# Late linear attention in 64-token chunks of two batches, fused with a cosine MLP

## The chip, the cores and the metric

The kernel runs on one core of one Trainium2 chip. The metric is the device time of the program in microseconds. TensorE (PE) does the matrix products, VectorE (DVE) and ScalarE (ACT) the elementwise work and the copies out of PSUM, GpSimd (POOL) part of the elementwise work that stays in SBUF, and the DMA queues of SyncE (SP), ACT and POOL move data.

## The reference

Two layers, one behind the other. The first is a linear attention with a decaying state, for 4 batches, 8 heads, 768 tokens and a head size of 48:

```python
for t in range(S):
    cur = u * k_t v_t^T
    y[t] = r_t (state + cur)
    state = w[:, None] * state + k_t v_t^T
```

The second takes its 3072 tokens of 384 values through an MLP of 2048 hidden values: `h = x @ w_in`, `g = h * cos(h)`, `out = g @ w_out`. The weights come as 64-bit floats.

## The kernel before

**Attention.** A batch's 768 tokens are cut into 6 chunks of C = 128; there are 24 chunks, taken round the batches, chunk `i` being batch `i % 4`, part `i // 4` (`chunk`, L656 on). In a chunk the decay is written as powers of w: k and r are multiplied by tables `decT_k` and `decT_r` (head dimension on partitions, time along the free axis, `spread_decay` L454, spread at L456), so that the scores of all pairs of tokens are plain products kT·rT (`mm_a` L815). A diagonal matrix with the bonus u goes into `A` on ACT (`diagonal` L805), and DVE writes the scores of earlier tokens over it (`mask` L825, a predicated copy). The chunk's output x, transposed, is the sum of the state read (`mm_x` L835, state `zt` against rT) and the values (`mm_x2` L845, v against A), in one PSUM bank; ACT and DVE copy it out as a high and a low half (`x_h`, `x_l`, L914, L919). The state product (`mm_z` L871, k against v) and its decay (`state` L926) make the state for the batch's next chunk. Heads are kept in pairs of 48 padded to 64 rows, so two score products stand on two halves of the array, four state reads and values on four strips of 32 columns. All of these are float32 products.

The first 12 chunks (XS) load k and r by tokens and transpose them on PE. The later ones ("late", `i >= XS`) load a second, staged copy of k and r and transpose it on DVE in 32x32 blocks (`load_s` L690, `tr_s` L735), and POOL applies the decay tables (`decay_s` L742). A late chunk issues its scores as one block on PE (`o_A` L821) and the state read, values and state product as a second (`mm_xz` L879).

**The tables.** `powers` (L442) takes w, transposed by PE, clamps it, forms 24 powers in seven multiplications, takes their reciprocals, and makes two factor tables `qk` and `qr` with one more product `cq`; DVE spreads both into `decT_k` and `decT_r`. PE transposes `decT_k` back into `dec_k` (tokens on partitions) for the state product. w is loaded by the first DMA on SP's queue (L430).

**The MLP.** Tokens go in 8 blocks of 3 chunks. One step takes a block and 128 of the 2048 hidden values: 9 products for h (`mm_h` L316, 384 columns, each operand split in a high and a low part), then on ACT and DVE the cosine (`whole` L327, `rest` L330, `cosine` L333), the gate g = h·cos(h) (`f_gate` L1030), and g's high and low halves (`f_gh` L1033, `f_gl` L1036), then 9 products for the output (`mm_o` L322). Blocks 0 to 3 walk the hidden dimension together in four groups, while their weights are converted (`conv` L564 on); blocks 4 to 7 take all of it at once and are stored once each.

**Order.** Nothing is issued in the order of the code. Each piece of work is an `Op` with an engine, a cost, a latency, a due time and the buffers it needs; `Plan.order` lays them out by a greedy pass, and repeats that with changed due times (PASSES = 60), replaying each order with random delays and keeping the best. A buffer is a `Buf` that takes one of several `Tile`s when its first user is placed; the eight PSUM banks are such tiles: `B_ACC` three, `B_H` two for h (three, `B_HX`, in the first four blocks), `B_ATT` three for late attention. While PE would idle ahead of the first score product, the plan puts warm-up matmuls on a zero tile (L1094).

## Time and profile before

| what | value |
|---|---|
| median of 3 runs (lowest, highest) | 512.46 us (512.25, 513.9) |
| the profiled execution's own time | 512.26 us |
| its span, first to last instruction | 510.5 us |
| mean granted PE clock | 0.999 |
| PE busy | 501.5 us, 98% |
| DVE busy | 381.0 us, 75% |
| ACT busy | 331.0 us, 65% |
| POOL busy | 177.1 us, 35% |

A row of the timeline has the start, the time from the first start to the last end, the engine, the line of the kernel, the operation, the tile written, the tiles read, the shapes, the count of merged instructions and, in brackets, the idle time before and what ended it. Weight loads of PE stand on rows of their own (PEld). A row of the windows has the window, its length, each engine's busy time with its count, the granted clock, the DMA share and the GB/s. A row of the groups has the count, the busy time and the mean of one in ns, then the idle time before.

### The profile page before, as it was taken

Reading aid. Unit: us, or ns where it says so; the run is one execution under the profiler, and the core shown is the slowest. Engines: PE = TensorE matmul, PEld = TensorE weight load, DVE = VectorE, ACT = ScalarE, POOL = GpSimd, SP = SyncE. Lnnn points to the kernel's source line nnn. Section 1 sums busy time; section 2 is a strip of 40 time slices with the busy share of each in tenths; the row PEclk is TensorE's granted clock in tenths of the full one; section 3 lists DMA queues with packets and bytes.
Section 4 is the critical chain, followed back from the end, with each engine's and each line's share of the span. In section 5 each row is a group of like instructions: output and inputs, shape, how many; then the busy total and the mean of one; then the engine's idle time right before and its main releaser. Section 6 shows DMA issues by size and latency. Waiting matters only on the chain.

```text
span 510.5 us, 11742 instructions
## 1 busy us (share of the span) xinstructions
PE 501.5 (98%) x4389; PEld 480.0 (94%) x4389; DVE 381.0 (75%) x773; ACT 331.0 (65%) x833; POOL 177.1 (35%) x184
## 2 busy tenths in 40 slices
PE   8999999999999999999999999999999999999995
PEld 5788899999999999999999999999999999999995
DVE  6898999888888875576777777777777767756553
ACT  2989987767667756556657465575665765655453
POOL 6777422445454451242426224224044041300000
PEclk9999999999999999999999999999999999999999
DMA  8999226586666593524676736446455465200001
GB/s 137 179 179 190 79 86 218 152 167 156 157 140 131 127 180 44 76 65 67 160 146 151 159 99 167 111 156 152 105 130 140 142 170 114 89 16 33 1 1 49
DMA packets 114975, 61.56 MB, mean 121 GB/s; under 512 B 78433, under 2 KB 110818, under 8 KB 114914
## 3 DMA queue, kind: packets, MB, share of 16 engines
q1 hardware_dynamic: 109586, 53.50, 42.7%
q0 software_dynamic: 5184, 7.08, 9.9%
q8 instruction: 35, 0.57, 0.5%
q14 instruction: 26, 0.21, 0.2%
q10 hardware_dynamic: 144, 0.20, 0.1%
HBM read 48.96 MB, written 11.80 MB: 119 GB/s over the span
## 4 chain that ended last, share of the span: by engine, by line
PE 94%; DMA 2%; DVE 1%; ACT 1%; issue 1%; POOL 0%; SPq 0%; DVEq 0%; POOLq 0%; ACTq 0%
PE bank L322 41%; PE bank L316 39%; PE bank L819 4%; PE bank L853 4%; PE bank L840 3%; PE bank L875 2%; PE bank L730 1%; DMA v<-in_v_dram 1%; DMA k<-in_k_dram 1%; ACT A L809 1%; PE bank L1094 0%; DVE pq L440 0%; POOL f L765 0%; DVE a L800 0%; DVE rq L447 0%
## 5 line engine op out<-in xcount | busy, mean ns | idle before, releaser
L322 PE MATMUL bank<-w_out_hi,gh 128*128 128x384 f32 x384 | 131.9, 344 | 0.0
L322 PE MATMUL bank<-w_out_hi,gl 128*128 128x384 f32 x384 | 129.8, 338 | 0.0
L316 PE MATMUL bank<-xh,w_in_lo 128*128 128x384 f32 x384 | 129.7, 338 | 0.0
L322 PE MATMUL bank<-w_out_lo,gh 128*128 128x384 f32 x384 | 129.5, 337 | 0.0
L316 PE MATMUL bank<-xh,w_in_hi 128*128 128x384 f32 x384 | 129.1, 336 | 0.0
L316 PE MATMUL bank<-xl,w_in_hi 128*128 128x384 f32 x384 | 128.8, 335 | 0.0
L330 DVE SCALAR_TENSOR_TENSOR f<-bank,qi 128x384 f32<-128x384 f32 (+1 forms) x132 | 71.4, 543 | 47.0 <-ACT qi L327 46.5
L327 ACT ACTIVATE qi<-bank 128x384 int32<-128x384 f32 (+1 forms) x132 | 62.8, 479 | 57.7 <-PE bank L316 57.0
L1033 ACT CAST gh<-f 128x384 fp32r<-128x384 f32 (+1 forms) x132 | 65.7, 500 | 48.9 <-DVE f L1030 46.9
L1030 DVE TENSOR_TENSOR f<-bank,f 128x384 f32<-128x384 f32 (+1 forms) x132 | 71.2, 542 | 32.5 <-ACT f L333 30.3
L1036 DVE TENSOR_TENSOR gl<-f,gh 128x384 fp32r<-128x384 f32 (+1 forms) x132 | 80.7, 613 | 19.6 <-ACT gh L1033 19.1
L333 ACT ACTIVATE f<-f 128x384 f32<-128x384 f32 (+1 forms) x132 | 67.3, 513 | 41.6 <-DVE f L330 40.8
L322 PEld LDWEIGHTS bank<-w_out_hi,gh 128*128 128x128 f32 x384 | 72.0, 188 | 3.0 <-issue 0.8
L316 PEld LDWEIGHTS bank<-xh,w_in_lo 128*128 128x128 f32 x384 | 72.2, 188 | 0.3 <-DVE w_in_lo L631 0.3
L316 PEld LDWEIGHTS bank<-xh,w_in_hi 128*128 128x128 f32 x384 | 72.2, 188 | 0.3 <-issue 0.2
L316 PEld LDWEIGHTS bank<-xl,w_in_hi 128*128 128x128 f32 x384 | 72.1, 188 | 0.0
L322 PEld LDWEIGHTS bank<-w_out_hi,gl 128*128 128x128 f32 x384 | 72.1, 188 | 0.0
L322 PEld LDWEIGHTS bank<-w_out_lo,gh 128*128 128x128 f32 x384 | 72.0, 188 | 0.0
L809 ACT ACTIVATE A<-ident,a 128x128 f32<-128x128 f32 x192 | 59.6, 391 | 4.9 <-DVE a L800 4.8
L743 POOL TENSOR_TENSOR kT<-kT,decT_k 112x512 f32<-112x512 f32 x12 | 15.6, 1301 | 129.3 <-DVE kT L738 74.4
L621 POOL TENSOR_TENSOR f<-f,raw 128x384 int32<-128x384 int32 x32 | 36.7, 1148 | 60.8 <-DVE f L610 31.7
L1078 POOL DMA_DIRECT2D out_dram<-f x36 | 32.7, 1012 | 40.6 <-DVE f L1030 17.2
(88 smaller groups left out, 589.5 us busy)
## 6 DMA issues: line engine op xcount, KB each, us to landing
raw<-in_moe_w_in_dram SPq DMA_DIRECT2D x32, 384.0 KB, 3.2
raw<-in_moe_w_out_dram SPq DMA_DIRECT2D x32, 384.0 KB, 3.2
out_dram<-f POOLq DMA_DIRECT2D x36, 192.0 KB, 4.5
k<-in_k_dram SPq DMA_DIRECT2D x24, 192.0 KB, 4.2
v<-in_v_dram SPq DMA_DIRECT2D x24, 192.0 KB, 5.1
raw<-in_k_dram SPq DMA_DIRECT2D x47, 96.0 KB, 3.1
raw<-in_r_dram SPq DMA_DIRECT2D x47, 96.0 KB, 2.1
out_dram<-f SPq DMA_DIRECT2D x23, 192.0 KB, 1.9
```

What stands on the lines that cost most here:

```text
L316: nc.tensor.matmul(ph, a, b_, start=(i == 0), stop=(i == len(mm) - 1))
L322: nc.tensor.matmul(acc, a[:, ts], b_[:, f, :], start=(first and i == 0), stop=(last and i == 2))
L327: nc.scalar.activation(qi, ph, AF.Copy, scale=INV_2PI, bias=0.25)
L330: nc.vector.scalar_tensor_tensor(q, ph, INV_2PI, qi, op0=ALU.mult, op1=ALU.subtract)
L333: nc.scalar.activation(q, q, AF.Sin, scale=TWO_PI, bias=0.5 * math.pi)
L621: lambda: nc.gpsimd.tensor_tensor(ai(), ai(), cn(), op=ALU.add),
L809: nc.scalar.activation(A[j]()[:, p, :], ident, AF.Copy, scale=ab()[:, h : h + 1])
L819: nc.tensor.matmul(cube(Ap[j])[:, p, :], kT()[ps, p, :], rT()[ps, p, :], start=True, stop=True)
L1030: nc.vector.tensor_tensor(g()[:, cs], ph()[:, cs], q()[:, cs], op=ALU.mult)
L1033: nc.scalar.copy(gh()[:, cs], g()[:, cs])
L1036: nc.vector.tensor_tensor(gl()[:, cs], g()[:, cs], f32(gh())[:, cs], op=ALU.subtract)
L1078: nc.gpsimd.dma_start(dst, ob(), accum_op=ALU.add)
```

## The change

**Late chunks.** A late chunk is now 64 tokens (CT) of two batches, laid side by side: batch 2m on partitions 0 to 63, batch 2m+1 on 64 to 127 where tokens are partitions, and one behind the other along the free axis where time runs there. There are still 12 late chunks of 128 columns of x. `late_chunk` is a function of its own. Its score product runs 16 matmuls of 64 columns, and the state product is issued right behind in the same PE block (`mm_az`); the second block (`mm_xx`) holds the state read, with 24 matmuls, and the values, with 32 in rounds that name each tile once. A state is needed after each 64 tokens, so only the last two late chunks leave it out. The two blocks write the same pair of banks (`P_ATT`, one `Tile` made of two parts), one after the other. Masks, diagonals and the update of the state work on the two batches at once; loads come in halves, one DMA for each batch. A second `dec_k` for 64 tokens is made once (`late_table`), and a 64-column diagonal and mask (`start_late`). An output tile of late chunks is stored by two DMAs, one for each batch's 64 rows.

**PSUM.** The eight banks are one tile; `B_H` has three for all blocks, `B_ATT` the two of the pair. The gate writes g over h in PSUM (`g = ph`) instead of an SBUF tile, and g's halves read it there.

**Tables.** `powers` makes 8 powers of w and 8 of its eighth power, and only 8 reciprocals; `decT_r` is spread by DVE, and `decT_k` is a mirrored copy of it by ACT. w is loaded on ACT's queue, ahead of ACT's table load. POOL's first product waits for `decT_r`.

**Plan.** The first six passes place everything; the 250 others change due times only of work that starts before 110 us, by single operations or by whole groups (a chunk, a weight, a step), and judge by PE's last end.

```diff
-PASSES = 60
+FULL = 6
+HORIZON = 110.0
+PASSES = 250
...
-        B_ACC, B_H, B_ATT = bank[0:3], bank[3:5], bank[5:8]
-        B_HX = bank[3:6]
+        P_ATT = [Tile(bank_all[:, 5:7], bank[5:7])]
+        B_ACC, B_H, B_ATT = bank[0:3], bank[3:5] + bank[7:8], bank[5:7]
+        B_HX = B_H
...
-            lambda: nc.sync.dma_start(wr[:, :, 0:D], w.rearrange("(p j) d -> p j d", j=2)),
+            lambda: nc.scalar.dma_start(wr[:, :, 0:D], w.rearrange("(p j) d -> p j d", j=2)),
...
-            for at, n in ((1, 1), (1, 2), (1, 4), (8, 1), (8, 2), (8, 4), (8, 8)):
-                last = at + n - 1
-                mul(pq[:, :, at + n : at + 2 * n], pq[:, :, at : at + n], pq[:, :, last : last + 1])
-            nc.vector.reciprocal(rq, pq)
-            mul(cq, pq[:, :, 15:16], pq[:, :, 7:8])
-            mul(qk, rq[:, :, 8:24], cq)
-            mul(qr, pq[:, :, 8:24], rq[:, :, 16:17])
+            mul(pe[:, :, 2:3], pe[:, :, 1:2], pe[:, :, 1:2])
+            mul(pe[:, :, 3:5], pe[:, :, 1:3], pe[:, :, 2:3])
+            mul(pq[:, :, 9:10], pe[:, :, 4:5], pe[:, :, 4:5])
+            mul(pe[:, :, 5:8], pe[:, :, 1:4], pe[:, :, 4:5])
+            for n in (1, 2, 4):
+                mul(pq[:, :, 9 + n : 9 + 2 * n], pq[:, :, 9 : 9 + n], pq[:, :, 8 + n : 9 + n])
+            nc.vector.reciprocal(pq[:, :, 0:8], pq[:, :, 16:8:-1])
...
-        o_dtk = op(DVE, -89, 0.65, lambda: spread_decay(nc.vector, decT_k, qk, rq), [o_pow], port=True)
-        o_dtr = op(DVE, -88, 0.65, lambda: spread_decay(nc.vector, decT_r, qr, pq), [o_pow], port=True)
+        o_dtr = op(DVE, -89, 0.65, lambda: spread_decay(nc.vector, decT_r, pq, pe), [o_pow0], port=True)
+        o_dtk = op(ACT, -88, 0.6, lambda: nc.scalar.copy(decT_k, decT_r[:, :, ::-1]), [o_dtr])
...
-                [l_r, l_k],
+                [l_r, l_k] + ([o_dtr] if i == 0 else []),
...
+            def mm_az():
+                for p in range(NP):
+                    for j in range(2):
+                        ps = slice(j * DP, j * DP + D)
+                        for b in range(2):
+                            nc.tensor.matmul(
+                                score(j)[half[b], p, :],
+                                late_t(kT)[ps, b, p, :],
+                                late_t(rT)[ps, b, p, :],
...
+                            nc.tensor.matmul(
+                                z[j * DP : j * DP + DP, b, p, :],
+                                kb()[half[b], 2 * p + j, :],
+                                vb()[half[b], 2 * p + j, 0:D],
...
+                def state():
+                    w_c = pq[0:KP, None, :, 16:17].to_broadcast([KP, 2, NP, D])
+                    nc.vector.tensor_tensor(zc[m], z_of()[0:KP], zc[m], op=ALU.add)
+                    nc.vector.tensor_tensor(zc[m], zc[m], w_c, op=ALU.mult)
+
+                last_z2[m] = op(DVE, due - 1.2, 1.2, state, [o_A, *o_zt, *before, o_pow], [sp])
...
+            def mm_xx():
+                x = xp()[:, :, 0 : NK * CT].rearrange("q b (kk t) -> q b kk t", kk=NK)
+                for kk in range(NK):
+                    for b in range(2):
+                        for g in range(4 * kk, 4 * kk + 4):
...
+                            nc.tensor.matmul(
+                                x[gs, b, kk, :],
+                                zb()[:, b, p, G * s : G * s + G],
+                                late_t(rT)[0:KP, b, p, :],
...
+                for group in rounds:
+                    for b in range(2):
+                        for g, n in group:
...
+                            nc.tensor.matmul(
+                                x[gs, b, g // 4, :],
+                                vb().rearrange("q h d -> q (h d)")[half[b], p * 2 * DP + at : p * 2 * DP + at + G],
+                                A[j]()[half[b], p, 0:CT],
...
-                g = ph if nt == 2 else q
+                g = ph
...
-                            nc.scalar.dma_start(dst, ob())
...
+                        for n, (rows, to) in enumerate(dst):
+                            if last and n == 0:
+                                nc.scalar.dma_start(to, ob()[rows])
+                            elif f0 == 0:
+                                nc.sync.dma_start(to, ob()[rows])
```

Where the instructions stand. PE's queue around one late chunk, before: the end of an output product of the MLP (L322), the scores (L819), one MLP step (left out), and the second block with state read (L840), values (L853) and state product (L875).

```order
L322 MATMUL bank_76<-w_out_lo,gh_113 128x384
L819 MATMUL bank_83<-rT_98,kT_94 128x128
L819 MATMUL bank_82<-rT_98,kT_94 128x128
...
L322 MATMUL bank_76<-w_out_lo,gh_114 128x384
L840 MATMUL bank_83<-rT_98,zt_124 32x128 x12
L853 MATMUL bank_83<-A_99,v_91 32x128 x2
L853 MATMUL bank_83<-A_100,v_91 32x128 x2
...
L875 MATMUL bank_82<-v_91,k_88 48x48 x8
L322 MATMUL bank_78<-w_out_hi,gh_112 128x384
```

The same place in the changed kernel, where L1070 are the scores, L1083 the state product, L1132 the state read and L1154 the values; the MLP's lines are L351 (h) and L357 (output).

```order
L357 MATMUL bank<-w_out_lo,gh_105 128x384
L1070 MATMUL bank<-rT_88,kT_86 64x64 x16
L1083 MATMUL bank<-v_81,k_78 64x48 x16
L357 MATMUL bank<-w_out_hi,gh_106 128x384
...
L357 MATMUL bank<-w_out_lo,gh_106 128x384
L1132 MATMUL bank<-rT_88,zt 32x64 x24
L1154 MATMUL bank<-A_91,v_81 32x64 x2
...
L1154 MATMUL bank<-A_92,v_81 32x64 x2
L357 MATMUL bank<-w_out_hi,gh_104 128x384
```

The state product moved from the end of the second block to the end of the first; between the blocks one MLP step (3 + 9 + 6 products) stands in both kernels.

DVE's queue behind the scores, before: the two masks (L826) between a gate (L1030) and the low half of a g (L1036), and the state update (L932, L933) three rows later.

```order
L1030 TENSOR_TENSOR f_107<-bank_79,f_107 128x384
L826 COPY_PREDICATED A_99<-upper,bank_83 128x512
L826 COPY_PREDICATED A_100<-upper,bank_82 128x512
L1036 TENSOR_TENSOR gl_116<-f_107,gh_113 128x384
...
L1036 TENSOR_TENSOR gl_117<-f_105,gh_114 128x384
L932 TENSOR_TENSOR zc_120<-bank_82,zc_120 112x192
L933 TENSOR_TENSOR zc_120<-zc_120,pq 112x192
```

After: the update (L1120, L1121) and the masks (L1102) in one piece, behind a gate (L1273) and ahead of the low half of a g (L1279).

```order
L1273 TENSOR_TENSOR bank<-bank,f_99 128x384
L1120 TENSOR_TENSOR zc_112<-bank,zc_112 112x384
L1121 TENSOR_TENSOR zc_112<-zc_112,pq 112x384
L1102 COPY_PREDICATED A_91<-upper_122,bank 128x4x64
L1102 COPY_PREDICATED A_92<-upper_122,bank 128x4x64
L1279 TENSOR_TENSOR gl_108<-bank,gh_105 128x384
```

The update moved ahead of the masks, and so between the two PE blocks.

DVE's queue at the start, before (from the reciprocal to the first transposed k and r) and after:

```order
L447 RECIPROCAL rq<-pq 128x96
L440 TENSOR_TENSOR cq<-pq 128x4
L440 TENSOR_TENSOR qk<-rq,cq 128x64
L440 TENSOR_TENSOR qr<-pq,rq 128x64
L456 TENSOR_TENSOR decT_k<-qk,rq 128x512
L456 TENSOR_TENSOR decT_r<-qr,pq 128x512
L781 TENSOR_TENSOR kT_94<-bank_82,decT_k 112x512
L755 TENSOR_TENSOR rT_96<-bank_83,decT_r 112x512
```

```order
L494 RECIPROCAL pq<-pq 128x4x8
L509 TENSOR_TENSOR decT_r<-pq,pe 128x512
L501 TENSOR_TENSOR pq<-pq 128x4x2
L781 TENSOR_TENSOR rT_88<-bank,decT_r 112x512
L807 TENSOR_TENSOR kT_86<-bank,decT_k 112x512
```

Three small products and one of the two spreads are gone, one small product for the state's decay is new, and rT comes ahead of kT.

More of the change, by code (lines that the diff above doesn't have):

```diff
@@ L90, in op @@
             self.lines[line] = o
+        o.group = self.group
         self.ops.append(o)
@@ L117, in _ready @@
                 return None
-            taken.add(id(best[1]))
+            taken.update(id(x) for x in best[1].parts)
             picks.append((b, best[1]))
@@ L136, in latest @@
             for b in o.bufs:
-                owners = tiles.setdefault(b.tile, [])
-                if not owners or owners[-1][0] is not b:
-                    if all(b is not x for x, _ in owners):
-                        owners.append((b, o))
+                for part in b.tile.parts:
+                    owners = tiles.setdefault(part, [])
+                    if not owners or owners[-1][0] is not b:
+                        if all(b is not x for x, _ in owners):
+                            owners.append((b, o))
         for owners in tiles.values():
@@ L167, in replay @@
                 port = end[o]
-        return max(end.values())
+        return max(end[o] for o in order if o.eng == "PE")
     def order(self, passes):
         best = None
+        for n in range(FULL):
+            order = self.one_pass(self.ops)
+            end = max(o.end for o in order)
+            if best is None or end < best[0]:
+                best = end, {o: o.due for o in order}, {o: o.start for o in order}
+            for o, t in self.latest(order).items():
+                o.due = t
@@ L178, in order @@
             if order is None:
-                self.change(rng, best)
                 continue
             draws = random.Random(2)
-            end = sum(self.replay(order, draws) for _ in range(6)) / 6
-            if best is None or end < best[0]:
-                best = end, {o: o.due for o in order}, max(o.end for o in order)
-            if n < 5:
-                for o, t in self.latest(order).items():
-                    o.due = t
-            else:
-                self.change(rng, best)
@@ L190, in order @@
-        return order
-    def change(self, rng, best):
-        spread, share = rng.choice((0.3, 1.0, 3.0)), rng.choice((0.1, 1.0))
-        for o, t in best[1].items():
-            o.due = t + (rng.gauss(0.0, spread) if t < 120 and rng.random() < share else 0.0)
-    def one_pass(self):
+            end = sum(self.replay(order, draws) for _ in range(4)) / 4
+            if low is None or end < low:
+                low = end
+                due = {o: o.due for o in ops}
+        for o in self.ops:
+            o.due = due.get(o, best[1][o])
@@ L787, in chunk @@
                 o_kd = op(e2, due - 2.7, c2, decay_k, [o_m, o_dk], [kb], port=True)
-            if not first and not late:
+            early_kd.append(o_kd)
+            if not first:
                 t_k = op(PE, due - 2.5, 0.49, tr(kTp, kb), [o_kd, o_pool], [kb, kTp, kT], lat=0.3)
```

469 lines of the change are left out of this document (317 added, 152 removed), and 4 rows, old and new, of the table rounds.

## The prediction

> **What bounds the kernel now.** I read the page first, then the windows by stage, then the timeline of TensorE (PE) around one late chunk, and last the first eleven microseconds on all engines. The page:
>
> ```profile
> span 510.5 us, 11742 instructions
> PE 501.5 (98%) x4389; PEld 480.0 (94%) x4389; DVE 381.0 (75%) x773; ACT 331.0 (65%) x833; POOL 177.1 (35%) x184
> PE 94%; DMA 2%; DVE 1%; ACT 1%; issue 1%; POOL 0%; SPq 0%; DVEq 0%; POOLq 0%; ACTq 0%
> ```
>
> The third line is the chain that ended last: 94% of it is PE. The windows of PE alone (busy, count, granted clock, DMA share, GB/s) show where PE is not the limit:
>
> ```profile
> 0.00:10.71 10.71, 8.32 (x53) 1.00 0.75 132
> 10.71:58.00 47.29, 45.96 (x888) 1.00 0.97 160
> 58.00:505.00 447.00, 447.00 (x3452) 1.00 0.48 116
> ```
>
> From 58 to 505 us PE has no idle time, so there only PE work counts. Before 10.71 (the first score product) its busy time is mostly warm-up on a zero tile; between 10.71 and 58 it idles 47.29 - 45.96 = 1.3 us. The profiled execution took 512.26 us: the span and 1.76 around it. It stands 0.2 below the median of the runs, 512.46; I make the sum against 512.26 and add the 0.2 at the end.
>
> The twelve late chunks lie in the last window, from 212.9 on. One of them, in PE's timeline:
>
> ```profile
> 213.10 1.16 PE L819 MATMUL bank<-rT,kT 48*128 48x128 f32 x16
> 214.19 0.44 PE L322 MATMUL bank<-w_out_hi,gh 128*128 128x384 f32 x1
> ...
> 217.27 0.34 PE L322 MATMUL bank<-w_out_lo,gh 128*128 128x384 f32 x1
> 217.54 0.86 PE L840 MATMUL bank<-rT,zt 112*32 112x128 f32 x24
> 218.22 1.08 PE L853 MATMUL bank<-A,v 128*32 128x128 f32 x32
> 219.23 0.56 PE L875 MATMUL bank<-v,k 128*48 128x48 f32 x16
> 219.72 0.45 PE L322 MATMUL bank<-w_out_hi,gh 128*128 128x384 f32 x1
> 220.01 0.34 PE L322 MATMUL bank<-w_out_hi,gl 128*128 128x384 f32 x1
> 220.18 0.34 PE L322 MATMUL bank<-w_out_lo,gh 128*128 128x384 f32 x1
> ```
>
> A matmul's own time overlaps its neighbours', so I cost by starts. Inside the MLP the next start comes 0.17 later (220.01 to 220.18). Score: 214.19 - 213.10 = 1.09. State read 0.68, values 1.01, state product 0.49. Each of the two blocks also stretches the MLP matmul before it (217.27 to 217.54 is 0.27) and behind it (219.72 to 220.01 is 0.29), together 0.2. So a late chunk costs PE 1.09 + 0.68 + 1.01 + 0.49 + 2 x 0.2 = 3.68 us, without the state product 3.19. From 212.9 to 505 us lie twelve chunks' scores (16 records each) and eight state products:
>
> ```profile
> L819 PE MATMUL bank<-rT,kT 48*128 48x128 f32 x192 | 13.9, 285 | 0.0
> L875 PE MATMUL bank<-v,k 128*48 128x48 f32 x128 | 4.5, 212 | 0.0
> ```
>
> So late attention costs 8 x 3.68 + 4 x 3.19 = 42.2 us of PE.
>
> **Part 1, late attention on PE.** A float32 matmul of the code shows as two records (12 in the code of L840, 24 above). What paces them? A narrow slice of the timeline, 217.53 to 217.56, holds this group; one reaching to 217.66 holds the same four and no more:
>
> ```profile
> 217.54 0.32 PE L840 MATMUL bank<-rT,zt 112*32 112x128 f32 x4
> ```
>
> Four records, one for each 32-column strip of the array, start within 0.03 us, then nothing until the strips are free. So a strip takes one record in 0.68 / 6 rounds = 113 ns (128 moving columns: 0.88 ns a column), and the four strips work side by side. The change halves the moving columns to 64 and doubles the tiles in use, except for the state read, which stays on four strips and gets twice the matmuls. Scores become 16 matmuls on four 64x64 tiles: 32 records, 8 rounds; the state product 32 records of 48 columns, 8 rounds; the state read 24 matmuls on four strips, 48 records, 12 rounds; the values 32 matmuls on eight 64x32 tiles, 64 records, 8 rounds. A round of 64 columns costs at least 64 x 0.88 = 57 ns. For the upper side I take L875 with its start and end: 0.49 / 8 rounds = 61 ns for 48 columns, so 75 ns for 64; and 43 to 61 ns for the state product. 28 rounds of 64 and 8 of 48: 1.94 to 2.59 us. To this come the two stretches of 0.2 and, inside the second block, a change of tile shape, 0 to 0.2. A chunk costs 2.34 to 3.2; without the state product 2.0 to 2.7. I take 2.95 and 2.5, nearer to the dear end, since no row shows eight tiles or a 64x64 tile. The product is now needed in 10 of 12 chunks: 10 x 2.95 + 2 x 2.5 = 34.5 (ends 27.4 and 37.4). The new table for the 64-token decay is 8 small transposes and a switch, 0.7 (L819, with as many matmuls of 128 columns, takes 1.09 and two switches; 0.3 to 1.3). Net 34.5 + 0.7 - 42.2 = **-7.0 us**, ends -14.5 and -3.5.
>
> Here a rule speaks against the change. The Trainium skill (TensorE: Matmul & The Clock Gate, section "Wait — 56ns, not 53.3ns?") says that start-to-start of matmuls never falls below about 25 ns, however few columns they have; four starts within 0.03 us disagree for one round, but no run here shows it for a long stream. By it the 176 records of a chunk would take 4.4 us instead of 2.55; this is a rival below.
>
> **Part 2, what stands around the late chunk.** The second block now reuses the two banks of the first, so it waits not for the two masks alone but for the state update as well, and DVE does the update ahead of the masks. DVE today, same chunk:
>
> ```profile
> 214.36 1.35 DVE L826 COPY_PREDICATED A<-upper,bank 128x512 f32<-128x512 int32 x2
> 218.32 0.56 DVE L1030 TENSOR_TENSOR f<-bank,f 128x384 f32<-128x384 f32 x1 [0.59 <-ACT f L333]
> 219.51 0.56 DVE L1036 TENSOR_TENSOR gl<-f,gh 128x384 fp32r<-128x384 f32 x1 [0.63 <-ACT gh L1033]
> 220.38 0.36 DVE L933 TENSOR_TENSOR zc<-zc,pq 112x192 f32<-112x192 f32 x1
> ```
>
> The update becomes two operations of 384 elements, 0.56 each as L1030; the masks halve to about 0.4 each: 1.9 us, plus up to 0.56 for an operation in progress. PE has one MLP step between the blocks, 217.54 - 214.19 = 3.35 with the stretches, 3.1 without. It fits with 0.6 to spare: cost 0. Queued behind the update and masks on DVE is the MLP's gl; PE needs it a step later. Beside a busy POOL the update's second half can be slower; in the first 60 us its mean was twice the 0.36 above:
>
> ```profile
> L933 DVE TENSOR_TENSOR zc<-zc,pq 112x192 f32<-112x192 f32 x6 | 4.6, 769 | 0.2
> ```
>
> Then 0.56 becomes some 1.2, the spare time is gone, and with other delays up to 0.4 is lost in each of 10 chunks, 4 us. g in PSUM keeps an h bank from the end of the gate to the end of gl, 218.88 to 220.07, 1.2 us longer; the three h banks come round after three MLP steps of about 3.1, 9.4 us, against a use of some 5: cost 0, hidden behind PE; were it not hidden, 1.2 a step would show at once as PE idle. More and smaller loads: the DMA share after 58 us is 0.48, and DVE is busy 75% of the span: 0.
>
> **Part 3, the head.** The chain of decay tables before the first score product:
>
> ```profile
> 0.94 0.85 SPq L430 DMA_DIRECT2D wr<-in_w_dram  x1
> 1.84 0.41 SPq L672 DMA_DIRECT2D k<-in_k_dram  x1
> ...
> 3.98 0.17 DVE L443 TENSOR_SCALAR pq<-bank 128x4 f32<-128x4 f32 x1 [2.80 <-PE bank L435]
> 4.18 1.43 DVE L440 TENSOR_TENSOR pq<-pq 128x4 f32<-128x4 f32 x7
> 5.65 0.75 DVE L447 RECIPROCAL rq<-pq 128x96 f32<-128x96 f32 x1
> 6.04 1.00 POOL L765 TENSOR_TENSOR f<-r,k 128x384 f32<-128x384 f32 x1 [2.17 <-DMA r<-in_r_dram]
> 6.32 0.74 DVE L440 TENSOR_TENSOR cq<-pq 128x4 f32<-128x4 f32 x1
> 7.37 0.69 DVE L456 TENSOR_TENSOR decT_k<-qk,rq 128x512 f32<-128x512 f32 x1
> 7.97 1.49 DVE L456 TENSOR_TENSOR decT_r<-qr,pq 128x512 f32<-128x512 f32 x1
> 9.38 0.68 DVE L781 TENSOR_TENSOR kT<-bank,decT_k 112x512 f32<-112x512 f32 x1
> 9.98 0.68 DVE L755 TENSOR_TENSOR rT<-bank,decT_r 112x512 f32<-112x512 f32 x1
> 10.71 1.16 PE L819 MATMUL bank<-rT,kT 48*128 48x128 f32 x16
> 11.15 2.45 ACT L809 ACTIVATE A<-ident,a 128x128 f32<-128x128 f32 x8 [1.86 <-DVE a L800]
> ```
>
> Seven multiplications stay seven: 0. The reciprocal goes from 96 to 32 elements: 0.75 to about 0.3, -0.45. cq, qk and qr go: 6.32 to 7.37, -1.05. The two tables, stretched to 1.49 beside POOL, become one of 0.69 (POOL's first product now waits for it), rT of 0.68 while ScalarE (ACT) mirrors the table, and kT of 0.68: 2.05 where 7.37 to 10.66 are 3.29, -1.25. The first score product comes 2.75 earlier, near 8.0. w on ACT's queue lets k's load start 0.9 earlier, at 0.94. For w itself it is between -0.5 (ACT issues a store in 0.38, below; SP took 0.85) and +0.5 if ACT is as much slower; I take 0.
>
> What is late next: POOL's product, then u (1.0 each), the reduction (0.56 like any pass over 384), ACT's diagonal (2.45) and a mask (0.68) end near 6.6 + 1.0 + 1.0 + 0.54 + 2.45 + 0.68 = 12.3 where today's first value product starts at 14.1: 1.8 is kept. Behind it the chain runs through loads:
>
> ```profile
> 16.05 5.10 DMA k<-in_k_dram
> 22.85 5.27 DMA v<-in_v_dram
> ```
>
> They start when PE frees a buffer, so they move along. The new order of the early part can at best win the 1.3 us of idle time too, and at worst lose the gain and 0.5. Head: **-1.8**, from -4 to +0.5.
>
> **Part 4, the end.** The last three chunks are stored as six half stores:
>
> ```profile
> 504.70 0.94 SPq L1076 DMA_DIRECT2D out_dram<-f  x2
> 505.76 0.38 ACTq L1074 DMA_DIRECT2D out_dram<-f  x1
> ```
>
> SP issues five of some 0.35: the last half goes out about 0.2 later than ACT's today. **+0.2**, 0 to 0.6.
>
> Sum: -7.0 - 1.8 + 0.2 = -8.6. 512.26 - 8.6 = 503.7, by the median 503.9.
>
> **The rivals.** *Issue-bound records (slower).* If PE can't start records faster on average than now, the change makes late attention dearer, since its records grow from 16 + 24 + 32 + 16 = 88 a chunk to 176. For it: L840, L853 and L875 all average 28 to 32 ns a record, with four strips or two. Against it: L819, with two tiles of 128 columns, needs 68, which a common limit wouldn't explain, and the four starts within 0.03. At 28 ns: 10 x (176 x 0.028 + 0.4) + 2 x (144 x 0.028 + 0.4) = 62.1, so +20.6 with the table, -1.6 for head and end: 531.5. The change breaks even at 18.7 ns a record ((42.2 - 0.7 + 1.6 - 4.8) / 2048 records). Chance 0.09. By the 25 ns of the Trainium skill (same page and section) it would be 56 us of late attention and 525.
>
> *The update holds the masks.* As priced, up to +4, with late attention at its dear end: 512.46 - 3.5 + 4 - 1.6 = about 511. Chance 0.05; a part of it is inside my range.
>
> *The change of order undoes the head*, and only late attention gains: 505.5 to 509.5. In the range.
>
> *Streaming alone sets the price*: late attention -12 or better and the whole head: below 499. Chance 0.06.
>
> **How the numbers follow.** My forecast with its bounds, 499 to 509.5: late attention from -10.5 to -3.5 with the head from -3 to +0.5. Chance 0.80. Outside: 0.09 issue-bound, 0.05 about 511, 0.06 below. About 0.3% (1.5 us) is what a measurement of this kernel can tell from no change. Faster by more: 0.80 + 0.06 = 0.86; within it 0.05, the case at 511; slower 0.09.
>
> **What would show it.** Right: the first score product near 8.0; a late score-and-state block of 0.8 to 1.2 us and a second block of 1.2 to 1.7, each from its start to the next MLP start; PE without idle time after 58 us; PE's records up, its span down. Wrong: values records at a steady 25 ns or more in place of bursts of eight; a wait of PE for DVE ahead of the state read in each late chunk; a first score product that is early while the chunks behind it wait for loads as long as now.

## The result, and the profile after

The changed kernel takes 510.22 us (median of 5 runs, 509.76 to 510.69); the kernel before, run beside it, 513.09 (5 runs, 512.25 to 513.9). Ratio 0.9946, 95% interval 0.9931 to 0.9961. The forecast was 503.9 with a range from 499 to 509.5: the direction was right, the size was not, and the time lies 0.7 us above the range. The profiled execution took 509.76 us, its span 508.0 against 510.5.

The page of the changed kernel: its span, the engines' busy time, the chain by engine.

```profile
span 508.0 us, 14010 instructions
PE 496.5 (98%) x5459; PEld 475.6 (94%) x5459; DVE 368.1 (72%) x775; ACT 328.4 (65%) x835; POOL 173.4 (34%) x186
PE 95%; DVE 1%; DMA 1%; POOL 1%; ACT 0%; issue 0%; POOLq 0%; DVEq 0%
```

PE has 1070 records more and is busy 5 us less. The windows of PE alone, cut at the first score product and at 58 us:

```profile
0.00:9.86 9.86, 7.38 (x46) 1.00 0.83 145
9.86:58.00 48.14, 45.91 (x889) 1.00 0.89 165
58.00:500.90 442.90, 442.90 (x4526) 1.00 0.49 113
```

After 58 us PE still has no idle time. Before that it idles 48.14 - 45.91 = 2.2 us behind the first score product, where it was 1.3. One late chunk in PE's timeline, with the MLP matmuls at its edges:

```profile
214.96 0.34 PE L357 MATMUL bank<-w_out_lo,gh 128*128 128x384 f32 x1
215.23 0.69 PE L1070 MATMUL bank<-rT,kT 48*64 48x64 f32 x32
215.74 0.64 PE L1083 MATMUL bank<-v,k 64*64 64x48 f32 x32
216.32 0.44 PE L357 MATMUL bank<-w_out_hi,gh 128*128 128x384 f32 x1
216.59 0.34 PE L357 MATMUL bank<-w_out_hi,gl 128*128 128x384 f32 x1
...
219.65 0.88 PE L1132 MATMUL bank<-rT,zt 112*32 112x64 f32 x48
220.45 0.86 PE L1154 MATMUL bank<-A,v 64*32 64x64 f32 x64
221.24 0.45 PE L357 MATMUL bank<-w_out_hi,gh 128*128 128x384 f32 x1
```

The score of one of the two chunks without a state product:

```profile
418.67 0.69 PE L1070 MATMUL bank<-rT,kT 48*64 48x64 f32 x32
419.29 0.44 PE L357 MATMUL bank<-w_out_hi,gh 128*128 128x384 f32 x1
```

By starts: score 0.51 us, state product 0.58, state read 0.80, values 0.79, and twice 0.2 for the stretched neighbours: 3.08 a chunk. Without the product the MLP follows the score directly, and the score takes 0.62: 0.62 + 0.80 + 0.79 + 0.4 = 2.61. 10 x 3.08 + 2 x 2.61 = 36.0, against 42.2 before. The second table, and the MLP around it:

```profile
74.49 0.34 PE L351 MATMUL bank<-xh,w_in_lo 128*128 128x384 f32 x1
74.76 1.09 PE L545 MATMUL bank<-ident,decT_k 128*64 128x128 f32 x16
75.78 0.44 PE L357 MATMUL bank<-w_out_hi,gh 128*128 128x384 f32 x1
```

From 74.76 to 75.78 it is 1.02, with the stretch 1.1. The end, on PE and on the queues that issue the stores:

```profile
500.58 3.54 SPq L1327 DMA_DIRECT2D out_dram<-f  x5
...
500.91 0.33 PE L357 MATMUL bank<-w_out_lo,gh 128*128 128x384 f32 x1
...
501.79 0.57 ACTq L1325 DMA_DIRECT2D out_dram<-f  x1
```

The last matmul starts 3.97 us earlier than before (504.88), but the span is only 2.5 shorter: SP needs 3.54 us for five half stores and ends at 504.12, 3.2 behind the last matmul. One by one, the five issues take 0.47, 0.60, 0.54, 1.06 and 0.59 us.

For the early part I went through PE's matmuls block by block: the start of a block less the work ahead of it, priced by the starts of the rows above and of the forecast (an MLP matmul 0.174, a score 0.136, a value 0.064). The difference is what PE has lost so far, by waits, warm-up and changes of tile shape. Before it is 10.0 us at 20 us, 11.4 at 60 and 11.5 at 80; after 9.1, 11.6 and 12.5; then it stays. So the new head is 0.9 ahead just before 20 us, and at 80 us the kernel is 1.0 behind.

Where the lead goes can be read from the traces. From 20 to 60 us PE idles 1.34 us where it idled 0.37. Two waits make the difference, both for a k that POOL has to decay before PE transposes it; the kernel before has no such wait there:

```profile
20.57 0.65 PE L772 MATMUL bank<-ident,k 128*112 128x128 f32 x4 [0.40 <-POOL k L799]
...
36.01 0.65 PE L772 MATMUL bank<-ident,k 128*112 128x128 f32 x4 [0.62 <-POOL k L799]
```

POOL starts the first product of a chunk (L791, before L765) 0.9 to 1.2 us earlier than before in the first three chunks, but no earlier in the fourth to sixth (18.42 against 17.69, 21.45 against 21.28, 26.02 against 25.91). The fourth, after and before:

```profile
18.42 1.00 POOL L791 TENSOR_TENSOR f<-r,k 128x384 f32<-128x384 f32 x1 [1.97 <-PE bank L880]
```

```profile
17.69 1.01 POOL L765 TENSOR_TENSOR f<-r,k 128x384 f32<-128x384 f32 x1 [0.95 <-DMA k<-in_k_dram]
```

Behind 60 us PE doesn't wait in either kernel, and yet 0.8 more is lost by 80. There each attention block that stands alone among MLP matmuls stretches its neighbours by 0.2, as in the late chunks. The changed kernel has five such blocks from 60 to 74 us (at 60.42, 62.23, 64.54, 67.99 and 71.97), the kernel before one, at 67.75, and the end of another: 1.0 against 0.3.

| term | forecast | measured |
|---|---|---|
| late attention on PE | -7.7 | -6.2 |
| second table | +0.7 | +1.1 |
| head and order, up to 80 us | -1.8 | +1.0 |
| end | +0.2 | +1.5 |
| sum | -8.6 | -2.6 (span: -2.5) |

### The profile page after: what moved, and what is told of

Same layout as the page of the kernel before. It is cut to its first block, busy times and chain, and to the rows that moved or that the text cites. A ratio compares the mean times of both kernels' runs of the same rounds, so it can differ in the third digit from the quotient of the medians.

```text
span 508.0 us, 14010 instructions
## 1 busy us (share of the span) xinstructions
PE 496.5 (98%) x5459; PEld 475.6 (94%) x5459; DVE 368.1 (72%) x775; ACT 328.4 (65%) x835; POOL 173.4 (34%) x186
## 3 DMA queue, kind: packets, MB, share of 16 engines
q0 software_dynamic: 5184, 7.08, 10.2%
## 4 chain that ended last, share of the span: by engine, by line
PE 95%; DVE 1%; DMA 1%; POOL 1%; ACT 0%; issue 0%; POOLq 0%; DVEq 0%
PE bank L357 41%; PE bank L351 39%; PE bank L880 2%; PE bank L846 2%; PE bank L1132 2%; PE bank L1154 2%; PE bank L772 2%; PE bank L1070 1%; PE bank L867 1%; DMA k<-in_k_dram 1%; PE bank L1083 1%; PE bank L902 1%; PE bank L1345 1%; POOL f L791 0%; POOL k L799 0%; DVE rT L781 0%
## 5 line engine op out<-in xcount | busy, mean ns | idle before, releaser
L357 PE MATMUL bank<-w_out_hi,gh 128*128 128x384 f32 x384 | 132.2, 344 | 0.0
L357 PE MATMUL bank<-w_out_hi,gl 128*128 128x384 f32 x384 | 129.8, 338 | 0.0
L351 PE MATMUL bank<-xh,w_in_lo 128*128 128x384 f32 x384 | 129.6, 337 | 0.0
L357 PE MATMUL bank<-w_out_lo,gh 128*128 128x384 f32 x384 | 129.4, 337 | 0.0
L351 PE MATMUL bank<-xh,w_in_hi 128*128 128x384 f32 x384 | 129.1, 336 | 0.0
L351 PE MATMUL bank<-xl,w_in_hi 128*128 128x384 f32 x384 | 128.7, 335 | 0.0
L1273 DVE TENSOR_TENSOR bank<-bank,f 128x384 f32<-128x384 f32 (+1 forms) x132 | 72.8, 551 | 39.0 <-ACT f L368 36.1
L1279 DVE TENSOR_TENSOR gl<-bank,gh 128x384 fp32r<-128x384 f32 (+1 forms) x132 | 71.1, 540 | 25.9 <-ACT gh L1276 25.5
L1276 ACT CAST gh<-bank 128x384 fp32r<-128x384 f32 (+1 forms) x132 | 61.6, 467 | 36.8 <-DVE bank L1273 35.1
L357 PEld LDWEIGHTS bank<-w_out_hi,gh 128*128 128x128 f32 x384 | 72.0, 187 | 2.5 <-DVE bank L1273 0.2
L351 PEld LDWEIGHTS bank<-xh,w_in_hi 128*128 128x128 f32 x384 | 72.1, 188 | 0.6 <-DVE A L853 0.2
L357 PEld LDWEIGHTS bank<-w_out_hi,gl 128*128 128x128 f32 x384 | 72.1, 188 | 0.3 <-DVE gl L1279 0.2
L351 PEld LDWEIGHTS bank<-xh,w_in_lo 128*128 128x128 f32 x384 | 72.2, 188 | 0.0
L351 PEld LDWEIGHTS bank<-xl,w_in_hi 128*128 128x128 f32 x384 | 72.1, 188 | 0.0
L357 PEld LDWEIGHTS bank<-w_out_lo,gh 128*128 128x128 f32 x384 | 72.0, 187 | 0.0
L695 POOL TENSOR_TENSOR f<-f,raw 128x384 int32<-128x384 int32 x32 | 36.3, 1135 | 62.3 <-DVE f L684 14.2
L836 ACT ACTIVATE A<-ident,a 128x128 f32<-128x128 f32 x96 | 29.4, 391 | 1.6 <-DVE a L827 1.5
```

What stands on the lines that cost most here:

```text
L351: nc.tensor.matmul(ph, a, b_, start=(i == 0), stop=(i == len(mm) - 1))
L357: nc.tensor.matmul(acc, a[:, ts], b_[:, f, :], start=(first and i == 0), stop=(last and i == 2))
L695: lambda: nc.gpsimd.tensor_tensor(ai(), ai(), cn(), op=ALU.add),
L836: nc.scalar.activation(A[j]()[:, p, :], ident, AF.Copy, scale=ab()[:, h : h + 1])
L1273: nc.vector.tensor_tensor(g()[:, cs], ph()[:, cs], q()[:, cs], op=ALU.mult)
L1276: nc.scalar.copy(gh()[:, cs], g()[:, cs])
```

## Experiments

Each group was run beside the kernel before on one chip. The median of before moved from group to group (512.72, 514.09, 513.19 and 513.74), so each time is given with its ratio to it. "Loss" is PE's loss at 80 us as above.

**1. The end.** First experiment: ACT issues both halves of the last chunk, POOL one half.

```diff
-                            if last and n == 0:
+                            if last:
                                 nc.scalar.dma_start(to, ob()[rows])
+                            elif jc == NJ - 2 and n == 1:
+                                nc.gpsimd.dma_start(to, ob()[rows])
```

> The changed kernel with the last stores spread: of the last three chunks' six halves SP issues three instead of five, GpSimd (POOL) one, ScalarE (ACT) two instead of one. Theory (the end waits for SP's five issues of 0.7 us each, the last ending 3.2 us behind the last matmul): the last issue ends near 502.9 instead of 504.12 and the span falls by 1.2, to about 509.0 us. Rival (the end is set by how long a store takes to land behind the last matmul, whoever issues it): the span stays within 0.3 of 508.0 and the time near 510.2.

Second: the last chunk as in the changed kernel, only POOL's half stays moved.

> The changed kernel with one half store moved, the second half of the last chunk but one, from SyncE's (SP) queue to GpSimd's (POOL): SP issues four halves, POOL one, ScalarE (ACT) one as before. In the first tail experiment ACT's two issues ended at 503.60, 2.6 behind the last matmul (501.02), and the span ended 6.2 behind it, against 7.1 in the changed kernel and 5.6 in the kernel before. Theory (the span ends 3.6 to 4.4 behind the end of the last issue, whoever issues): SP's fourth issue ends near 503.1, so the span ends 5.8 to 6.4 behind the last matmul, 0.7 to 1.3 less than in the changed kernel: about 509.2 us by medians, 509.5 if the profile overstates it. Rival (the landing of the last half behind the last matmul sets it): 7.1 as in the changed kernel, 510.2.

And the changed kernel again, beside the second:

> The changed kernel once more, beside the other kernels of this call on the same chip, as their yardstick. If its time is a property of the kernel: 509.8 to 510.7 us, the last matmul near 500.9, the span end near 7.1 behind it.

The queues at the end, of the first experiment:

```profile
500.70 1.75 SPq L1329 DMA_DIRECT2D out_dram<-f  x3
501.73 0.59 POOL L1327 DMA_DIRECT2D out_dram<-f  x1 [66.50 <-DVE f L1315]
501.90 1.70 ACTq L1325 DMA_DIRECT2D out_dram<-f  x2
```

Its last issue ends at 503.60 (expected 502.9: ACT's second half took 1.1, not 0.6), the span at 507.2, 6.2 behind the last matmul (501.02) instead of 7.1. The second: SP ends at 504.74, not near 503.1, since its fourth issue took 1.29; the span ends at 508.3, 6.3 behind the last matmul (501.93). The changed kernel again: SP ends at 504.82, the span at 508.4, 7.3 behind (501.10). In all of these the span ends 3.5 to 3.9 us behind the last issue, whoever issues; before it was 4.4. That is the theory's term, at 0.9 instead of 1.2. The span ends 1.8 us behind the landing of the last store (506.27 in the changed kernel, 505.39 in the first experiment, 508.77 before). The landing comes 4.4 to 5.5 us behind the last matmul in these four, so the rival, a fixed time from matmul to landing, falls. The medians show less: 510.11 (ratio 0.9950, 0.9937 to 0.9963), 510.05 (0.9922, 0.9903 to 0.9941) and, the changed kernel, 510.67 (0.9941, 0.9920 to 0.9963); the intervals overlap, so 0.9 us is shown in the profiles and not proved by the times.

**2. What paces a late matmul.** The same score matmuls, one tile of the array after the other:

```diff
-                for p in range(NP):
-                    for j in range(2):
-                        ps = slice(j * DP, j * DP + D)
-                        for b in range(2):
+                for j in range(2):
+                    for b in range(2):
+                        ps = slice(j * DP, j * DP + D)
+                        for p in range(NP):
```

> The changed kernel with the late score products in another order of the same matmuls: all four pairs of one 64x64 tile of the array one after the other, then the next tile, instead of going round the four tiles. Theory (a tile takes a record of 64 columns only every 55 to 60 ns, and the 16 ns a record of the changed kernel come from four tiles at work side by side): 32 records take 1.4 to 1.9 us instead of 0.51, in twelve chunks 11 to 16 us more: 521 to 526 us. Rival (PE issues records at a fixed pace, whatever tile they go to): 0.51 us a chunk as before and 510.2 us; by a pace of 25 ns 0.8 us, 513.7.

PE's timeline of this kernel, the first block of a chunk:

```profile
216.43 1.36 PE L1070 MATMUL bank<-rT,kT 48*64 48x64 f32 x29
217.58 0.27 PE L1083 MATMUL bank<-v,k 64*64 64x48 f32 x3
...
217.75 0.22 PE L1070 MATMUL bank<-rT,kT 48*64 48x64 f32 x1
217.79 0.63 PE L1083 MATMUL bank<-v,k 64*64 64x48 f32 x23
218.35 0.45 PE L357 MATMUL bank<-w_out_hi,gh 128*128 128x384 f32 x1
```

The 32 records spread over 217.79 - 216.43 = 1.36 us, 42 ns each on average, where they took 16; the state product, on other tiles, already fits between the last of them. The block is 1.92 us instead of 1.09, 10.0 us in twelve chunks; the time is 520.97 (1.0134, 1.0108 to 1.0159), 10.3 above the changed kernel run beside it. The rival, one pace for all records, falls: order alone makes the same records 2.6 times dearer. The theory stands, and so does its size: record by record, the starts on one tile lie 58 ns apart in both kernels (216.536, 216.594, 216.653 here). In the changed kernel four tiles start within 20 ns, and the next four 58 ns behind (215.333, 215.392, 215.450). Here the next tile starts 0.29 us behind the one before, when that has started five of its eight records, so two tiles overlap in part; that is why 32 records take 1.36 us and not the 1.4 to 1.9 expected.

**3. The head.** w back first on SP's queue; POOL's first product really held back until the table is there:

```diff
-            lambda: nc.scalar.dma_start(wr[:, :, 0:D], w.rearrange("(p j) d -> p j d", j=2)),
+            lambda: nc.sync.dma_start(wr[:, :, 0:D], w.rearrange("(p j) d -> p j d", j=2)),
...
+                if i == 0:
+                    n0.tensor_copy(heads(mb)[0:1, 0:1, 0:1], decT_r[0:1, 0:1, 0:1])
                 n0.tensor_tensor(heads(mb), rn(), kb()[:, :, 0:D], op=ALU.mult)
```

> The changed kernel with the head as the prediction took it, in an unchanged order: the load of w is issued first on SyncE's queue instead of ScalarE's, and GpSimd's first product really waits for the decay table (it first copies one element of it). Both theories: w's transpose starts near 3.7 instead of 4.51, the power products take 0.15 to 0.2 each beside an idle GpSimd, the table 0.69 instead of 1.14, and the first score product starts near 8.0 instead of 9.86. Theory (what is behind the first score product runs by loads, buffers and GpSimd, not by the tables): at most 0.4 us of it is left at the end, 509.8 to 510.4. Rival (the prediction's: of an earlier table most is kept): 1.5 to 1.9 us faster, about 508.5.

The changed kernel's head, all engines, for comparison:

```profile
0.91 1.29 ACTq L473 DMA_DIRECT2D dec_k<-in_w_dram  x1
...
4.51 0.22 PE L479 MATMUL bank<-ident,dec_k 4*128 4x4 f32 x1
...
5.17 1.04 POOL L791 TENSOR_TENSOR f<-r,k 128x384 f32<-128x384 f32 x1 [1.32 <-DMA r<-in_r_dram]
...
5.38 0.85 DVE L484 TENSOR_TENSOR pq<-pe 128x4 f32<-128x4 f32 x1
...
7.27 1.14 DVE L509 TENSOR_TENSOR decT_r<-pq,pe 128x512 f32<-128x512 f32 x1
...
7.82 0.65 PE L772 MATMUL bank<-ident,k 128*112 128x128 f32 x4 [0.54 <-DMA k<-in_k_dram]
...
9.86 1.16 PE L846 MATMUL bank<-rT,kT 48*128 48x128 f32 x16
```

And that of the experiment:

```profile
0.94 0.87 SPq L473 DMA_DIRECT2D dec_k<-in_w_dram  x1
...
1.20 3.38 PE L1351 MATMUL bank<-warm 128*128 128x256 bf16 x15 [1.20 <-DVE dec_k L464]
...
4.51 0.26 PE L479 MATMUL bank<-ident,dec_k 4*128 4x4 f32 x1
...
5.42 0.17 DVE L484 TENSOR_TENSOR pq<-pe 128x4 f32<-128x4 f32 x1
...
6.63 0.69 DVE L509 TENSOR_TENSOR decT_r<-pq,pe 128x512 f32<-128x512 f32 x1
...
8.04 0.68 DVE L813 TENSOR_TENSOR kT<-bank,decT_k 112x512 f32<-112x512 f32 x1
...
8.74 0.65 PE L772 MATMUL bank<-ident,k 128*112 128x128 f32 x4 [0.31 <-DMA k<-in_k_dram]
...
9.76 1.16 PE L852 MATMUL bank<-rT,kT 48*128 48x128 f32 x16
```

With POOL held back the power product takes 0.17 instead of 0.85 and the table 0.69 instead of 1.14, as expected, and both factors are ready at 8.72. The two other expectations missed. w's transpose doesn't move, because fifteen warm-up matmuls stand ahead of it on PE until 4.58; their number comes from the plan. And the first score product stays at 9.76, because the second chunk's k transposes stand ahead of it and wait for that chunk's load. 510.54 us (0.9959, 0.9946 to 0.9972), last matmul 501.46, loss 13.1: no gain. The next kernel takes both away:

```diff
+        order = [o for o in order if o not in first_k[1]]
+        at = order.index(first_A[0]) + 1
+        order[at:at] = first_k[1]
...
+                    n = 11 if o is o_wT else 5 if o is o_tt else n
```

> The kernel of the head experiment with two more changes of what stands ahead of the first score product on TensorE (PE), the rest of the order unchanged: the warm-up matmuls ahead of w's transpose are 11 instead of 15 (those ahead of the table's transposes 5), and the second chunk's k transposes with their decay on VectorE stand behind the first score product instead of ahead of it. In the head experiment w's transpose came at 4.51 as before, straight behind the fifteenth warm-up, and the first score product at 9.76, because the k transposes ahead of it waited for the second chunk's k until 8.74. Both theories: w's transpose near 3.7, first score product near 8.0. Theory (the head's loss is what stands ahead on PE, and what follows the first score product moves with it): the last matmul comes 1 to 1.5 us earlier than in the head experiment (501.46), so about 500.2, and the time is near 509.2. Rival (the chunks behind run by loads and GpSimd): the last matmul stays within 0.4 of 501.4, the time near 510.4.

w's transpose came at 3.66, and the first score product still at 9.58: now r's transposes and the table's stood ahead. The first chunk's k had landed only for a start of 5.16, since its load was issued behind w's. The second chunk's score product fell back to 13.26 (12.39 in the changed kernel), and the last matmul to 502.37; 511.34 us (0.9949, 0.9930 to 0.9968), loss 13.5. Both expectations failed on the start of the first score product. Both tables are ready at 7.12 here, but rT starts at 7.76, behind r's transposes (6.67), and the score stands behind the table's transposes (8.59). Where w's, k's and r's chains meet on PE, shortening one gave little, and this exchange in the order had its price behind.

**4. The order.** The search charged for each change of PE between MLP and attention:

```diff
+            if o.eng == 'PE':
+                t += 0.3 if o.mlp != mlp else 0.0
+                mlp = o.mlp
```

> The changed kernel with one thing added to the search that orders the early part: its replay charges 0.3 us for each change of TensorE (PE) between MLP and attention. The order found has 8 such changes before MLP alone is left, where the changed kernel has 20. Theory (each change costs 0.1 us or a little less, and the loss of 1.0 us between 60 and 75 us is that): 0.8 to 1.2 us faster than the changed kernel, about 509.2 us, with the same first score product near 9.9. Rival A (changes cost nothing, the early part is held by loads and decay tables): no difference, 510.2. Rival B (the alternation hid waits for VectorE): slower by 0.5 or more.

The search left out (`PASSES = 0`):

> The changed kernel with the random search left out: only the six full passes order the work; 14 changes between MLP and attention. Theory (the changes count, the search itself earned little): 0.3 to 0.8 us faster than the changed kernel, about 509.7. Rival (the search earned what it was made for): 1 us slower or more, 511.2 or above.

Other start values of the search (`random.Random(1)`, `(2)`, `(3)`), with the end of the first tail experiment:

> The changed kernel with another start value (1 instead of 9) of the random search that orders the early part, and the last stores spread as in the first tail experiment (SP three halves, POOL one, ACT two). The work of TensorE (PE) is the same, so the start of its last matmul shows what the early part lost: 500.9 to 501.9 in four profiles of the changed kernel's order so far, 500.9 less the 1.0 that the early part lost against the kernel before would be 499.9. Theory (the order that the search happens to draw sets the early part's loss): the three draws and the fourth order of this call differ by over 1 us in their last matmul and one comes to 500.3 or less, with a time near 508.8. Rival (the new head, table and half loads cost what they cost, in any order): all of them within 500.7 to 502.

> As the first draw, start value 2. Theory and rival as there: a spread of over 1 us between the four, or all last matmuls within 500.7 to 502. Its order has 16 changes between MLP and attention against 12 in the first draw; if the changes alone set the loss it is 0.4 slower than that one.

> As the first draw, start value 3, 14 changes between MLP and attention. Theory and rival as there.

And a charge of 0.15, with that end:

> The changed kernel (start value 9) with 0.15 us charged in the search's replay for each change between MLP and attention, where the earlier experiment charged 0.3, and the last stores spread. 12 changes. That experiment saved 0.2 us between 60 and 75 us but lost 0.9 between 30 and 45. Theory (the order as a whole decides, by its waits; a milder charge loses less there): a last matmul between 500.2 and 501.2, a time of 508.6 to 509.8. Rival (the charge misleads the search): 501.6 or later, 510.4.

| kernel | time | ratio, interval | loss at 20, 60, 80 us | last matmul |
|---|---|---|---|---|
| charge 0.3 | 511.41 | 0.9978, 0.9965 to 0.9990 | 9.6, 12.5, 13.3 | 501.63 |
| no search | 511.95 | 0.9991, 0.9978 to 1.0003 | 9.4, 14.2, 15.2 | 503.50 |
| draw 1 | 510.29 | 0.9943, 0.9922 to 0.9964 | 11.6, 13.6, 14.3 | 502.64 |
| draw 2 | 509.74 | 0.9936, 0.9911 to 0.9960 | 8.8, 11.9, 12.7 | 501.03 |
| draw 3 | 510.89 | 0.9957, 0.9939 to 0.9976 | 8.7, 12.4, 13.2 | 501.71 |
| charge 0.15 | 510.76 | 0.9948, 0.9931 to 0.9966 | 8.7, 13.4, 14.0 | 502.31 |

My theory fell in its first form: with under half the changes the time came out as rival B said, slower. The loss is 0.8 larger, of which 0.9 arises before 60 us; behind it, where two attention blocks stand among the MLP instead of six (the second table counted in both), only 0.1 is saved, since PE there waits 0.33 us for a mask of DVE (at 66.27). The search does earn something: without it the last matmul comes 2.6 later. And no draw comes below 501.0, so nothing speaks for bad luck of one start value: in six other orders of the same work the loss is 0.2 to 2.7 more than in the changed kernel's. Small differences in it say nothing, though: four profiles of the changed kernel's own order have their last matmul at 500.91, 501.02, 501.10 and 501.93. The draws spread by more than 1 us, as my theory had it, but none came to 500.3, and the charge of 0.15 came out as its rival said. (Draw 1's profile holds 7 us of halved clock, last section.) The waits for POOL's decayed k stand in all these profiles with an undisturbed clock, 0.5 to 2.2 us in sum from 20 to 80 us. Draw 2 with the spread stores is the best version found, 509.74 us: better than before, not shown to be better than the changed kernel.

**5. Parts alone.** Open was then whether head, search or the late part's operations bring the loss. The kernel before with the new head's lines (`o_w`, `powers`, `decT_r`, `decT_k`):

> The kernel before with the new head alone: w on ScalarE's queue, the powers in fewer steps with one reciprocal of 32, one decay table and its mirrored copy. Late attention, stores and search as before (60 passes over everything). Yardstick: the kernel before, last matmul at 504.88, 512.46. The prediction's view (head -1.8): last matmul near 503.1, 510.7. Theory (what lies behind the first score product runs by loads, buffers and GpSimd): within 0.5 of 504.9, 512.5. Rival (the new head itself makes the early part dearer, by table and copies): 505.5 or later, 513.2.

With the new class `Plan` and its groups:

> The kernel before with the new search alone: six full passes, then 250 that move the part of the plan before 110 us, by single operations or by groups, scored by the last end on TensorE (PE). Theory (the search is worth as much as the old one, and the loss of 1.0 us comes with the new operations of the late part): last matmul within 0.5 of 504.88, 512.5. Rival (the new search finds the worse order, 1.0 us of it, as between 60 and 75 us of the changed kernel): 505.6 or later, 513.3. The other way, it finds a better one: 504.2 or earlier.

With both:

> The kernel before with the new head and the new search together, which is the changed kernel without 64-token late attention, g in PSUM and half stores. If the two add up: the sum of their differences to 504.88. Theory (neither is worth anything at the end): 504.4 to 505.4, 512.5. If the loss of 1.0 us in the early part comes from head and search in whatever mix: 505.6 or later, 513.3. The prediction's view: 503.1, 510.7.

And the changed kernel with the head's lines of before:

> The changed kernel with the old head: w on SyncE's queue, seven power products, a reciprocal of 96, two decay tables of VectorE. Yardstick: the changed kernel, last matmul at 500.91 to 501.10, 510.2 to 510.7. Prediction's view (the new head gains 1.8): 502.7 or later, 512.2. Theory (little of the head reaches the end): within 0.7 of 501.0, 510.5. Rival (the new head is the loss in the early part): 500.2 or earlier, 509.6.

| kernel | time | ratio, interval | loss at 20, 60, 80 us | last matmul |
|---|---|---|---|---|
| before + head | 514.75 | 1.0032, 1.0016 to 1.0047 | 8.8, 13.0, 13.6 | 507.08 |
| before + search | 513.95 | 1.0005, 0.9992 to 1.0018 | 12.0, 14.8, 15.5 | 508.84 |
| before + both | 513.94 | 1.0010, 0.9991 to 1.0030 | 11.7, 14.6, 15.0 | 508.37 |
| after, old head | 513.87 | 1.0010, 0.9998 to 1.0022 | 10.2, 13.3, 14.0 | 503.72 |

(The profiles of the second and third hold a stretch of halved clock, so only their times count.) The new head alone makes the kernel before slower by 0.3%, as the rival had it: it is 1.2 us ahead at 20 us and 2.1 behind at 80. PE's waits from 8 to 80 us come to 4.1 us there, against 2.2 in the kernel before. The two largest (total, count, longest):

```profile
PE bank L826 <- ACT kT L797: 1.4, 2, 0.8
PE bank L479 <- ACT decT_k L471: 1.2, 1, 1.2
```

The copies of kT by ACT, which PE waits for here, belong to chunks behind the first two; in the kernel before they cost 0.2, and the wait for `decT_k` 0.7. The new search alone changes nothing, both together nothing that can be told from zero. Yet the old head in the changed kernel costs 0.69% (1.0010 against 0.9941, 3.5 us), as much as the prediction's view and more. Of this, 1.3 lie between 90 and 170 us, where MLP matmuls start up to 0.37 us late; the profile shows only 0.2 of it as a wait. So the parts don't add: the same head is worth +1.6 us in one order and -3.5 in another, and the order changes with it. What adds, within what these times can tell, is the late part. The changed kernel against "before + both" is 0.9946 / 1.0010, 3.3 us less, give or take some 1.3 by the two intervals; by the table of terms late attention, second table and end give -6.2 + 1.1 + 1.5 = -3.6.

## Why the forecast was wrong, point by point

Of the 6 us between the forecast sum and the measured one, the head is 2.8, late attention 1.5, the end 1.3 and the second table 0.4. The step that failed first is Part 3's "1.8 is kept"; two more terms were mis-sized, the values in Part 1 and the issues in Part 4.

- **Bound, right.** PE is the limit after 58 us; its MLP keeps its pace, and no late wait of PE appears.
- **Part 1, right in mechanism; the gain came out a fifth short.** A chunk took 3.08 us and 2.61 without the product, where I took 2.95 and 2.5. The step that failed is the price of the values: I gave eight 64x32 tiles the round of four strips (57 to 75 ns). Measured: score 8 rounds in 0.51 us, 64 ns; state read 67; values 0.79, 99 ns a round, and still 85 without the 0.11 that a score, too, takes longer when the MLP follows it. The first 32 records of the values start within 0.24 us, eight every 56 ns, as priced; the other 32 take 0.40, and no run shows why. That the sum of a chunk is only 0.1 off is partly luck: score and state read lay below the dear end that I took for them. The second table cost 1.1 instead of 0.7.
- **The issue-bound rival, wrong.** The 176 records of a chunk take 2.68 us, 15.2 ns each, below the 18.7 ns at which the change would break even; the values are at 12.3. The floor of 25 ns between starts in the Trainium skill (TensorE: Matmul & The Clock Gate, section "Wait — 56ns, not 53.3ns?") doesn't hold for streams over several tiles here; that page's section "Part 3: Packing small matmuls — row/col tiling" lets tiles overlap, and experiment 2 agrees.
- **Part 2, right.** The state update ahead of the masks costs PE nothing, nor does g in PSUM: no wait of PE after 58 us.
- **Part 3, wrong in its steps and its conclusion.** "POOL's first product now waits for it": that wait stands only in the plan, and no semaphore carries it; POOL started at 5.17, made one power product 0.85 and the table 1.14. (The description of the change above has the same error.) w on ACT's queue: I took 0; ACT issued in 1.29 us where SP took 0.85, and its transpose moved from 3.68 to 4.51, the time that the plan's warm-up matmuls now end. The first score product came at 9.86, not 8.0. But the conclusion failed too: "1.8 is kept". I followed the chain to the first value product and took what lies behind it to move along. Even the 0.9 us that the head was ahead at 20 us were gone by 60: POOL's products of the fourth to sixth chunk came no earlier, and PE waited 1.0 us for the k that POOL decays, a chain that has no term in my sum. Another 0.8 went behind 60 us by stretched neighbours, which I didn't price for the early chunks. Experiment 5 shows that this is no rule of the head alone but of the order around it. I had allowed the order to "lose the gain and 0.5"; it lost the gain and 1.0.
- **Part 4, mis-sized.** Five issues "of some 0.35" took 0.47 to 0.60 us and one of them 1.06: a store of half the rows took SP longer to issue than a whole one did before (0.34). +1.5 instead of +0.2, shown by the ends of issue, landing and span in experiment 1.

What stays open: whether some order lets POOL's chain follow the head, so that its gain lasts. Ten orders with the new head were run; none kept it. That PE's waits for POOL cost the lead is read from the traces; no run took them away.

## What to carry to other kernels

Price a shortened start-up chain at nothing until the profile shows that the work behind it moves along: where several loads and an order found by search meet, look at what stands ahead on the in-order engine, not at what the data allow. Small matmuls on several tiles of the array gain from going round the tiles; measure the round for each number of tiles. Each block of them that stands alone among large matmuls cost 0.2 us here, so count the blocks as well. And when stores are cut into pieces, count the issues on each queue behind the last matmul.

## What the runs showed of the hardware, unexpected

**The clock halves without a long gap.** Draw 1's profile, PE in windows of 1 us (busy, count, granted clock, DMA share, GB/s):

```profile
7.00:8.00 1.00, 0.71 (x7) 1.00 1.20 213
8.00:9.00 1.00, 0.36 (x3) 1.00 1.22 171
9.00:10.00 1.00, 0.41 (x4) 1.00 1.28 166
...
11.00:12.00 1.00, 1.00 (x9) 0.50 1.06 119
...
17.00:18.00 1.00, 1.00 (x24) 0.64 0.63 126
18.00:19.00 1.00, 1.00 (x37) 1.00 0.91 174
```

PE was busy 1.48 of 3 us, its longest gap 0.93, and from 11 to 17.6 us the clock was 0.50; a score product of 1.16 took 2.08. In the changed kernel it is 1.73 of these 3 us, and the clock stays at 1.00. The busy share alone doesn't decide, though: with the search left out PE is busy 1.49 us from 8 to 11 (0.15, 0.62 and 0.72), its longest gap is 0.96, and the clock stays at 1.00 too. The Trainium skill (TensorE: Matmul & The Clock Gate, section "Part 1: The HAM clock gate (the "warmup" mystery)") puts the drop down to an idle window of about 3.4 us; here it came with no gap over 0.93. What decides is open.

**Issuing a store** took 0.33 to 0.38 us for a whole tile and 0.47 to 0.60 for half its rows, on SP, ACT and POOL alike. In each profile with half stores, one of the last two issues took longer: 1.06 us of SP in the changed kernel, 1.10 of ACT in the first experiment, 1.56 of SP in the changed kernel's second run. In 17 of the 18 profiles the span ends 1.8 us behind the landing of the last store (in draw 1's, 3.8).
